# The order of the three part products in the split matmuls of a gated mix of linear attention and Fourier mixing

## The chip, the cores and the metric

The kernel runs on one core of one Trainium2 chip, in one launch. The metric is the device time of that core in microseconds (us). A profile is one execution of the program recorded by the hardware profiler; its engines are PE (TensorE matmuls), PEld (TensorE loads of stationary operands), DVE (VectorE), ACT (ScalarE), POOL (GpSimd) and SP (SyncE, which issues most DMAs).

## The reference

The inputs are `x` of 2048 tokens by 576 features, weights for a linear attention with 32 heads of 18 features, and two pairs of DFT matrices (over the sequence, 2048 x 2048, and over the features, 576 x 576). Cut to what matters:

```python
g = sigmoid((x * gate_w).sum(-1, keepdims=True))
# a: linear attention
q, k, v = split(x @ wqkv)
pq, pk = phi(q), phi(k)                  # t + 1 or exp(t)
kv = einsum("bhsd,bhse->bhde", pk, v)
z = einsum("bhsd->bhd", pk)
a = (einsum("bhqd,bhde->bhqe", pq, kv) / einsum("bhqd,bhd->bhq", pq, z)) @ wo
# b: Fourier mixing, the real part of a DFT over D and then over S
re = einsum("bsd,ed->bse", x, dft_hid_re)
im = einsum("bsd,ed->bse", x, dft_hid_im)
b = einsum("ts,bse->bte", dft_seq_re, re) - einsum("ts,bse->bte", dft_seq_im, im)
return g * a + (1 - g) * b
```

All of it is float32.

## The kernel before, in words

**Split operands.** A matmul here takes operands of the type float32r. To keep float32 precision, each operand is written as a high part (a copy rounded to that type, made by ScalarE in `hi_of`, L167) and a low part (the rest, made by VectorE in `lo_of`, L177). A product of two such operands is then three part products that add up in the same PSUM bank: high x high, high x low and low x high. `FULL` (L608) lists them in this order; the first number of a pair picks the part of the stationary operand, the second that of the moving (streamed) one. Each matmul has 128 rows, 128 columns of the stationary operand and 288 streamed columns (half of 576), except the rest of the feature dimension (below).

**Stages.** The attention comes first: key features (L512 and L197), the key-weight sums (L637), the query features and the attention output (L197 again), up to 264 us of the span. In the key features' first stage (L512), for each weight row, four matmuls stream that same row under four different stationary tiles, one for each of four token tiles. In L197 (`steps`) each contraction chunk gives high high, high low, low high, and the last chunk two matmuls, 14 in all. In L637 each of the three part products runs for both halves of 576 columns before the next, so two matmuls in a row have the same stationary tile.

Then the Fourier part runs twice, with the real and then with the imaginary matrices, and both runs have the same two steps. Each uses a fast scheme with seven products of half-sized blocks instead of eight (`PRODUCTS`, `ORDER`).

1. *The products over D* (`Hidden.run`, with `Hidden.product`; matmuls at L903). For each of 8 tiles `p` and each of the seven products there are seven matmuls into one bank: two contraction chunks `c` with three part products each, and one rest matmul of 96 rows, in which the leftover 32 features stand with their parts stacked. The stationary operand is a tile of `x` (`xf` or `xb`, high and low in the same tile), the moving one the weight `w` (`wf`, where the high and low parts of both chunks come by one transfer, L872). VectorE and ScalarE combine the seven results into the factors of the next step: a high part `fh` and a low part `fl` for each tile `p` and each form `f` (class `Factors`). For the last two tiles (6 and 7) this split is put into `backlog`, and done when the sequence products already run: ScalarE makes the high parts in batch 1, VectorE the low parts after that (`rest_lows` in batch 2).

2. *The sequence products* (`sequence`; matmuls at L1058). There are 32 batches `n`, four for each of 8 pairs of output rows. A batch covers two tiles `p` (2b and 2b + 1, where b is n modulo 4) and has, for each of the seven products and each of the two tiles, three part products: 42 matmuls. The stationary operand is a piece of the DFT matrix, `c` (high and low parts, made batch by batch), the moving one the factors. In the last pair of rows of the second run two batches are taken together. After the fourth batch of a pair the seven banks are combined, mixed with the attention rows and stored.

**What sets the order.** The order of instructions on PE, VectorE, ScalarE and SP is written out by hand in these stages: it is the order of the program text. Low parts are often put off (`lo_later`, `tick`), so that they stand behind other work of VectorE.

The lines that the change touches are L608 (beside which a second list is added), L900 in `product` and L1057 in `sequence`.

Of the kernel before, what the change touches and what calls it, by code (L numbers as in the profile page):

```python
# [14 lines left out]
P = 128  # L15
# [38 lines left out]
class Ring:  # L54
# [5 lines left out]
    def next(self):  # L60
        self.n += 1
        return self.at[(self.n - 1) % len(self.at)]
# [63 lines left out]
def kernel(  # L126
# [23 lines left out]
    def at(offset, shape, dtype=F, name="t"):  # L150
        count[0] += 1
        t = nc.alloc_sbuf_tensor_at(f"{name}_{count[0]}", list(shape), dtype,
                                    offset=base + offset)
        return t.ap()
# [8 lines left out]
    def bank():  # L163
        return psum.tile([P, 512], F, tag="bank", name="bank")
# [17 lines left out]
    def tick():  # L182
        while pending:
            pending.pop(0)()

    def add(dst, a, b, op=ALU.add):
        nc.vector.tensor_tensor(out=dst, in0=a, in1=b, op=op)  # L187
# [6 lines left out]
    def run(ps, pairs):  # L194
        pairs = list(pairs)
        for n, (a, b) in enumerate(pairs):
            nc.tensor.matmul(ps, a, b, start=(n == 0), stop=(n == len(pairs) - 1))  # L197

    def half(h):
        return slice(h * HALF, (h + 1) * HALF)  # L200
# [283 lines left out]
    for h in range(2):  # L484
        ps = [bank()[:, :HALF] for _ in range(FT)]
        parts = wkt.split(h, KC)
        for c, (raw, hi, lo) in enumerate(first):
            passes = [(hi, c), (lo, c), (hi, 5 + c)][:3 if c < KC else 2]
            tiles = [range(FT)] * len(passes)
            if h == 0 and c == 0:  # L490
                a, b = ab
# [114 lines left out]

    wvt, wot, gts = {}, [], {}
    FULL = ((0, 0), (0, 1), (1, 0))  # L608
    kv = [bank() for _ in range(3)]

    def kv_of(g):
# [16 lines left out]
    for c in range(5):  # L628
        ps = [bank(), bank()]
        passes = FULL if c < KC else FULL[:2]  # L630
        for q in range(NCU):
# [137 lines left out]
    def build_m(gs):  # L769
        for g in gs:  # L770
            n = gsize(g)
            for h in range(2):
                ps = bank()
                run(ps[:n, :HALF], [(kvb[:n, g, a, :n], wot[g][:n, b, half(h)])
                                    for a, b in FULL])
                nc.scalar.activation(mf[:n, g, half(h)], ps[:n, :HALF], AF.Copy)
# [86 lines left out]
    class Hidden:  # L863
# [33 lines left out]

        def product(self, ps, p, k, start):
            x, (w, wl) = self.x[p, k], self.w[k]
            ops = [(x[:, a, c * P:c * P + P], w[:, 2 * c + b]) for c in range(2) for a, b in FULL]  # L900
            ops.append((self.rest[p][:96, 6 - k], wl[:96]))
            for n, (a, b) in enumerate(ops):
                nc.tensor.matmul(ps, a, b, start=(start and n == 0), stop=(n == len(ops) - 1),  # L903
                                 skip_group_check=True)
# [112 lines left out]
    def sequence(m, g, src, dst, last=None, between=None):  # L1017
        late, held, stores, rest_lows = [], [], [], []
        for n in range(NP * NB):
            j, b = divmod(n, NB)  # L1020
            if b == 0:
                ps = {k: bank()[:, :HALF] for k in PRODUCTS}
                row = {t: at(mix_ring.next(), [P, D], F, "row") for t in (j, j + NP)}
                for t, a in row.items():
                    nc.sync.dma_start(out=a, in_=src[t])
            c = m.ready.pop(0)
            m.load(n + 3)
            while stores:
                stores.pop(0)()
            if n == 2:  # L1030
                tick()
            if m.raws:
                new = m.make()
                next(new)
                next(new)
                if b < NB - 1:
                    next(new, None)
            else:
                new = iter(())
                tick()  # L1040
            if n == 1:
                while backlog:
                    backlog.pop(0)()
                rest_lows += pending[-2:]
                del pending[-2:]
            elif n == 2:
                while rest_lows:
                    rest_lows.pop()()
            end = last is not None and j == NP - 1
            held.append((b, c))  # L1050
            if end and b == NB - 2:
                continue
            for q, (l, f) in PRODUCTS.items():
                for b, c in held:
                    for k in range(BS):
                        p = b * BS + k
                        for i, (x, y) in enumerate(FULL):  # L1057
                            nc.tensor.matmul(ps[q], c[x][:, l, k], factors[p](y, f),  # L1058
                                             start=(p == 0 and i == 0),
                                             stop=(p == NP - 1 and i == 2))  # L1060
            held.clear()
            if between is not None:
                between(n)
            while late:
                late.pop(0)()
            if b < NB - 1:
                continue
            y = at(Y_AT, [P, 2, 2, HALF], F, "ys")
            c11, c12, c21, c22 = (y[:, i // 2, i % 2] for i in range(4))

            def mix(t, v, h=None, g=g, row=row, store=True, end=end):
                cs = slice(0, D) if h is None else half(h)
                a = row[t][:, cs]
                nc.vector.scalar_tensor_tensor(a, v, g[:, t:t + 1], a, op0=ALU.mult, op1=ALU.add)  # L1074
                if store:
                    stores.append(lambda: nc.sync.dma_start(out=dst[t][:, cs], in_=a))
                if store and end:
                    stores.pop()()

            nc.scalar.activation(c11, ps[1], AF.Copy)  # L1080
            tick()
            add(c12, ps[6], c11, ALU.subtract)
            add(c11, ps[2], c11)
            next(new, None)
            if end:
                mix(j, c11, 0)
                add(c21, c12, ps[7], ALU.subtract)
                add(c12, ps[5], c12)
                add(c22, c12, ps[7], ALU.subtract)
                mix(j + NP, c22, 1)  # L1090
                mix(j + NP, c21, 0, store=False)
                mix(j, c12, 1, last, store=False)
                mix(j, ps[3], 1)
                mix(j + NP, ps[4], 0, last)
            else:
                add(c21, c12, ps[7], ALU.subtract)
                add(c12, ps[5], c12)
                add(c22, c12, ps[7], ALU.subtract)
                add(c12, ps[3], c12, ALU.subtract)
                add(c21, c21, ps[4], ALU.subtract)  # L1100
                late += [lambda t=t, i=i, y=y, mix=mix: mix(t, y[:, i].rearrange("p a b -> p (a b)"))
                         for i, t in enumerate((j, j + NP))]
        for f in late:
            f()
        for f in stores:
            f()
# [84 lines left out]
    mr.load(0)  # L1191
    first.run(mr, {1: 5, 2: 6, 6: 7}, {0: 5, 1: 6, 3: 7})
    sequence(mr, gate_n, att, mid, between=late)
    factors.clear()
    second.run(mi, {1: 5, 2: 6, 6: 7}, {0: 5, 1: 7})
    sequence(mi, gate_m, mid, [out[t * P:(t + 1) * P] for t in range(NT)], last=gate_n)
    paced.close()

# [87 lines left out]
```

## Time and profile before

| What | Value |
|---|---|
| Median of 3 runs | 733.61 us (733.57 to 733.9) |
| Span of the profiled execution | 730.4 us |
| Runs over the span | 3.2 us |
| Mean granted TensorE clock | 1.000 |
| PE instructions | 5,444 matmuls, 5,444 weight loads |
| Products over D, in the chain of waits | 264.15 to 316.8 us, and 501.1 to 548.3 us |
| Sequence products, in the chain of waits | 316.8 to 495.4 us, and from 548.3 us to the end |
| DMA traffic | 158.82 MB, mean 217 GB/s |

The times of runs are of executions without the profiler. The page of the profile gives no time of its own for the profiled execution but its span, from the first to the last instruction; the 3.2 us between this and the median of the runs lie outside of the span.

A row of a group reads: line, engine, operation, output tile <- input tiles, shape, count | busy us, mean ns of one | idle time of the engine just before. A matmul's duration there (some 295 ns) is longer than the distance from one start to the next, since matmuls overlap; the price of one matmul is read from a stretch: its length by its count. In a row of the timeline or of the chain stand the start in us, the length in us, and what ran, with the count of instructions that were merged. In a row of waits stand who waited, for whom, and the total, the times and the longest in us.

### The profile page before, as it was taken

To read this page: it belongs to the slowest core of one execution; us is meant where nothing else is said; L and a number is where in the kernel's file an instruction comes from. 1 tells how busy PE (TensorE), PEld (TensorE's weight loads), DVE (VectorE), ACT (ScalarE), POOL (GpSimd) and SP (SyncE) were. 2 spreads that over 40 slices of the span, in tenths; PEclk is the share of its full clock that TensorE was granted. 3 is DMA by queue.
4 is the path that set the end of the run, shared out by engine and by line. 5 is a ranking of instruction groups with operands and counts; after the bars stand their busy time and mean duration, and the time that the engine had idled before them with its cause. 6 is when DMAs were issued, how large, how long until landed. Compare 5 with 4: busy or idle time off the path is not lost.

```text
span 730.4 us, 13876 instructions
## 1 busy us (share of the span) xinstructions
PE 724.2 (99%) x5444; PEld 722.4 (99%) x5444; DVE 601.0 (82%) x995; ACT 335.6 (46%) x522; POOL 57.0 (8%) x98
## 2 busy tenths in 40 slices
PE   8999999999999999999999999999999999999998
PEld 8999999999999999999999999999999999999997
DVE  5689866779999948989899989767889988788884
ACT  6898435678644444453344334323535332232231
POOL 1011200051032110000000000000000000000000
PEclk9999999999999999999999999999999999999999
DMA  7286787677477999644475666889964544544440
GB/s 254 84 275 217 265 296 234 226 215 224 155 221 298 362 312 383 211 153 135 165 240 177 228 233 202 296 279 395 374 219 130 171 145 135 156 149 148 152 152 33
DMA packets 54356, 158.82 MB, mean 217 GB/s; under 512 B 6420, under 2 KB 11092, under 8 KB 53268
## 3 DMA queue, kind: packets, MB, share of 16 engines
q1 hardware_dynamic: 45044, 118.90, 48.7%
q0 software_dynamic: 8960, 38.65, 14.6%
q8 instruction: 43, 0.70, 0.4%
q10 hardware_dynamic: 288, 0.39, 0.2%
q14 instruction: 21, 0.17, 0.1%
HBM read 115.05 MB, written 41.39 MB: 214 GB/s over the span
## 4 chain that ended last, share of the span: by engine, by line
PE 96%; DMA 2%; DVE 1%; ACT 0%; issue 0%; SPq 0%; DVEq 0%
PE bank L1058 48%; PE bank L197 23%; PE bank L903 14%; PE bank L637 7%; PE bank L512 2%; PE bank L738 1%; DMA wraw<-in_wk_dram 1%; DMA wf<-wm 1%; DMA craw<-in_xg_dram 1%; PE bank L619 0%; DVE row L1074 0%; ACT xb L167 0%; DVE ys L187 0%; PE bank L622 0%; ACT wd L167 0%
## 5 line engine op out<-in xcount | busy, mean ns | idle before, releaser
L1058 PE MATMUL bank<-fh,c 128*128 128x288 f32 x1792 | 357.5, 295 | 0.0
L1058 PEld LDWEIGHTS bank<-fh,c 128*128 128x128 f32 x1792 | 287.5, 188 | 0.0
L1058 PE MATMUL bank<-fl,c 128*128 128x288 f32 x896 | 264.2, 295 | 0.0
L167 ACT ACTIVATE c<-craw 128x1792 fp32r<-128x1792 f32 (+1 forms) x84 | 121.4, 1447 | 187.1 <-DVE craw L187 166.3
L1058 PEld LDWEIGHTS bank<-fl,c 128*128 128x128 f32 x896 | 168.9, 189 | 0.0
L177 DVE TENSOR_TENSOR c<-craw,c 128x1792 fp32r<-128x1792 f32 (+4 forms) x86 | 142.0, 1653 | 5.9 <-ACT c L167 5.7
L187 DVE TENSOR_TENSOR craw<-craw 128x256 f32<-128x256 f32 (+1 forms) x192 | 98.3, 512 | 25.2 <-DMA craw<-in_ci_dram 12.7
L197 PE MATMUL bank<-wd,xs 128*128 128x288 f32 (+1 forms) x784 | 106.3, 296 | 0.4 <-ACT wd L167 0.4
L197 PEld LDWEIGHTS bank<-wd,xs 128*128 128x128 f32 x784 | 104.7, 188 | 0.6 <-ACT wd L167 0.6
L903 PE MATMUL bank<-wf,xf 128*128 128x288 f32 x588 | 92.1, 297 | 0.2 <-DMA wf<-wm 0.2
L903 PEld LDWEIGHTS bank<-wf,xf 128*128 128x128 f32 x588 | 84.0, 189 | 0.4 <-issue 0.4
L197 PE MATMUL bank<-mw,qs 128*128 128x288 f32 x448 | 63.2, 297 | 0.0
L637 PE MATMUL bank<-pk,c 128*128 128x288 f32 x448 | 61.1, 296 | 0.1
L637 PEld LDWEIGHTS bank<-pk,c 128*128 128x128 f32 x448 | 59.9, 189 | 0.3 <-DVE c L177 0.3
L197 PEld LDWEIGHTS bank<-mw,qs 128*128 128x128 f32 x448 | 59.9, 188 | 0.2 <-DVE qs L177 0.2
L187 DVE TENSOR_TENSOR ys<-bank,ys 128x288 f32<-128x288 f32 x63 | 28.8, 457 | 16.1 <-PE bank L1058 12.4
L336 DVE SCALAR_TENSOR_TENSOR acc<-bank,e 128x288 f32<-128x288 f32 x64 | 28.3, 454 | 15.2 <-ACT e L335 13.7
L177 DVE TENSOR_TENSOR fl<-fl,fh 128x864 fp32r<-128x864 f32 (+1 forms) x32 | 34.6, 1093 | 7.1 <-ACT fh L167 5.8
L167 ACT ACTIVATE fh<-fl 128x864 fp32r<-128x864 f32 (+1 forms) x32 | 29.8, 950 | 16.2 <-DVE fl L187 16.2
L903 PE MATMUL bank<-wf,xr 96*128 96x288 f32 x112 | 33.3, 298 | 0.0
L1123 ACT ACTIVATE acc<-bank,gate 128x288 f32<-128x288 f32 x32 | 16.0, 500 | 35.1 <-PE bank L197 34.8
L187 DVE TENSOR_TENSOR ys<-ys,bank 128x288 f32<-128x288 f32 x47 | 21.2, 450 | 12.6 <-PE bank L1058 12.0
(107 smaller groups left out, 665.9 us busy)
## 6 DMA issues: line engine op xcount, KB each, us to landing
xf<-xm SPq DMA_DIRECT2D x42, 512.0 KB, 7.9
craw<-in_cr_dram SPq DMA_DIRECT2D x32, 512.0 KB, 4.1
craw<-in_ci_dram SPq DMA_DIRECT2D x32, 512.0 KB, 3.5
xraw<-in_xa_dram SPq DMA_DIRECT2D x28, 320.0 KB, 4.3
xm<-xb POOLq DMA_DIRECT2D x8, 1024.0 KB, 5.9
wf<-wm SPq DMA_DIRECT2D x14, 576.0 KB, 5.4
xr<-xr SPq DMA_DIRECT2D x14, 448.0 KB, 8.0
xm<-xb POOLq DMA_DIRECT2D x8, 768.0 KB, 5.9
```

The lines of the kernel that those rows point to most:

```text
L167: return nc.scalar.activation(dst, src, AF.Copy, bias=bias)
L177: nc.vector.tensor_tensor(out=dst, in0=src, in1=hi, op=ALU.subtract)
L187: nc.vector.tensor_tensor(out=dst, in0=a, in1=b, op=op)
L197: nc.tensor.matmul(ps, a, b, start=(n == 0), stop=(n == len(pairs) - 1))
L336: nc.vector.scalar_tensor_tensor(dst, ps, 0.0, e, op0=ALU.max, op1=ALU.add)
L512: nc.tensor.matmul(ps[i], x[:, i * P:(i + 1) * P], wkt.row(h, j), start=(c == 0 and n == (0 if h or i < 2 else 2)), stop=(c == KC and n == 1))
L637: nc.tensor.matmul(ps[h][:, :HALF], t[:, a, k], pk[s][:, b, half(h)], start=(s == 0 and n == 0), stop=(s == NT - 1 and n == len(passes) - 1))
L738: nc.tensor.transpose(banks[c // KC][:, (c % KC) * P:(c % KC + 1) * P], a, ident)
L903: nc.tensor.matmul(ps, a, b, start=(start and n == 0), stop=(n == len(ops) - 1), skip_group_check=True)
L1058: nc.tensor.matmul(ps[q], c[x][:, l, k], factors[p](y, f), start=(p == 0 and i == 0), stop=(p == NP - 1 and i == 2))
L1123: done.append(nc.scalar.activation(acc[i][:, half(h)], ps[:, :HALF], AF.Copy, scale=gate[:, i:i + 1]))
```

## The change

A second list, `TURN`, has the same three part products with the first two exchanged: high low, high high, low high. The products over D use it for both chunks of every product. The sequence products use it in all batches but the first of each run (`n` is 0 there, and `b` is 0 too as no other batch is held). Everything else is as it was.

```diff
     FULL = ((0, 0), (0, 1), (1, 0))
+    TURN = ((0, 1), (0, 0), (1, 0))
...
         def product(self, ps, p, k, start):
             x, (w, wl) = self.x[p, k], self.w[k]
-            ops = [(x[:, a, c * P:c * P + P], w[:, 2 * c + b]) for c in range(2) for a, b in FULL]
+            ops = [(x[:, a, c * P:c * P + P], w[:, 2 * c + b]) for c in range(2) for a, b in TURN]
...
                         p = b * BS + k
-                        for i, (x, y) in enumerate(FULL):
+                        for i, (x, y) in enumerate(TURN if n or b else FULL):
                             nc.tensor.matmul(ps[q], c[x][:, l, k], factors[p](y, f),
                                              start=(p == 0 and i == 0),
                                              stop=(p == NP - 1 and i == 2))
```

## The prediction

> **What bounds the kernel now.** The first view is the page's table of busy time, with the slices under it.
>
> ```profile
> PE 724.2 (99%) x5444; PEld 722.4 (99%) x5444; DVE 601.0 (82%) x995; ACT 335.6 (46%) x522; POOL 57.0 (8%) x98
> PEclk9999999999999999999999999999999999999999
> ```
>
> TensorE works for 99% of the span of 730.4 us, in 5,444 matmuls with as many weight loads, and its granted clock is full in every slice. VectorE follows at 82%. Busy time on PE is modelled, so the second view is the chain of waits, in order of time. Its pieces say how long a stretch of matmuls took from its start to what followed, and so what one of them costs.
>
> ```profile
> 21.13 44.55 PE bank L197 x336
> 65.67 19.17 PE bank L637 x144
> 130.90 2.09 PE bank L637 x16
> 264.15 52.63 PE bank L903 x392
> 316.79 178.61 PE bank L1058 x1344
> 495.39 0.02 issue
> 495.41 5.60 DMA wf<-wm
> 501.01 0.14 issue
> 501.14 47.15 PE bank L903 x350
> 548.29 175.38 PE bank L1058 x1320
> ```
>
> The two stretches of L1058 (the sequence products) and of L903 (the products over D), which the change touches, make up 178.61 + 175.38 + 52.63 + 47.15 = 453.8 us of the chain. One sequence product matmul takes 178.61 / 1344 = 132.9 ns in the first run and 175.38 / 1320 = 132.9 ns in the second. The third view is who waited for whom, on PE.
>
> ```profile
> PE bank L223 <- POOL ones_f L219: 1.2, 1, 1.2
> PE bank L512 <- ACT wd L167: 0.6, 1, 0.6
> PE bank L197 <- ACT wd L167: 0.4, 1, 0.4
> PE bank L903 <- DMA wf<-wm: 0.2, 1, 0.2
> ```
>
> That is 2.4 us in all, none of it in L1058. The 5.60 us of a transfer in the chain lie under other matmuls; PE stood for 0.2 us of it. So in the touched stages the time is the number of matmuls times the price of one. A reordering can act only through that price, or through a wait which comes earlier.
>
> **The change, part by part.** Nothing is added or removed. Line 900 gives 7 products x 8 tiles x 2 chunks x 2 runs = 224 triples. Line 1057 gives 42 matmuls in each of 31 batches (all but the first) in each of 2 runs: 2,604 matmuls, or 868 triples. Together 1,092 triples, 3,276 matmuls, change their order from high high, high low, low high to high low, high high, low high. In the built program these swaps and the waits that go with them are all that differs; the rows of VectorE, ScalarE, GpSimd and of both DMA-issuing engines stand in the same order.
>
> The groups by form show that the work per matmul stays:
>
> ```profile
> L1058 PE MATMUL bank<-fh,c 128*128 128x288 f32 x1792 | 357.5, 295 | 0.0
> L1058 PE MATMUL bank<-fl,c 128*128 128x288 f32 x896 | 264.2, 295 | 0.0
> L1058 PEld LDWEIGHTS bank<-fh,c 128*128 128x128 f32 x1792 | 287.5, 188 | 0.0
> L1058 PEld LDWEIGHTS bank<-fl,c 128*128 128x128 f32 x896 | 168.9, 189 | 0.0
> ```
>
> Every matmul has its own load of the stationary operand, also where it repeats the one before (the first two of a triple share c high in both orders): 1,792 + 896 loads for 2,688 matmuls. The loads of high, high, low come in the same order as before. What moves is the streamed factor: high, low, high becomes low, high, high. So the second and third matmul of a triple now stream the same tile one after the other. The price of such a repeat is the first unknown.
>
> *Its bounds.* The nearest row is the stage at L512, where four matmuls in a row (one for each of four token tiles) stream the same weight row under different stationary tiles. Its stretch without a wait, from the timeline:
>
> ```profile
> 13.29 7.84 PE L512 MATMUL bank<-wd,xs 128*128 128x288 f32 x58
> ```
>
> With one duration of 0.29 us taken off for the last matmul's own length, (7.84 - 0.29) / 57 = 132.4 ns from start to start. Three of four pairs there repeat the streamed operand, and it is no dearer than the stages that hardly repeat it: 132.6 at L197 (44.55 / 336) and 132.9 at L1058. The dearest stretch with whole tiles and no rest rows among the quoted is L637, 19.17 / 144 = 133.1 ns. So the price of the changed matmuls lies between 0.5 ns under and 0.2 ns over today's: over all 3,276 of them, -1.6 to +0.7 us. I take the row that it is nearest to, L512, for the matmul that becomes a repeat: 1,092 x -0.5 ns = -0.5 us. L903 has 134.3 ns (52.63 / 392), with rest matmuls of 96 rows after every six whole ones; those stay where they are.
>
> The Trainium skill, "TensorE: Matmul & The Clock Gate", section "Back-to-back issue gap", gives N / 2.4 + 2.5 ns for an isolated warm matmul, which is an estimate of 122.5 ns for 288 columns, 10.4 ns below this trace's 132.9. If a repeated streamed operand got rid of that whole difference, 1,092 repeats would bring 11.4 us and the time would be 722; the L512 stretch, at 132.4 ns, speaks against it.
>
> *The waits.* In the old order the low factor is read by the second matmul of a triple, now by the first, one matmul (0.13 us) sooner. In the products over D, low and high weights come with the same transfer, so nothing changes there. In the sequence products the low factors of the last two tiles are made late, by VectorE, shortly before batch 3 reads them. A low factor that came too late would hold up every matmul behind it, since PE's matmuls start in program order all through the trace, and the products' readers on ScalarE and VectorE in turn. The start of batch 3 is 126 matmuls after the first start of L1058:
>
> ```profile
> L1058 PE MATMUL bank<-fh,c x1792: 292/295/302, 316.6 to 726.6; 128*128 128x288 f32 x200
> 331.40 2.32 DVE L177 TENSOR_TENSOR fl<-fl,fh 128x1152 fp32r<-128x1152 f32 x2
> 333.26 0.43 PE L1058 MATMUL bank<-fh,c 128*128 128x288 f32 x2
> 334.72 0.29 PE L1058 MATMUL bank<-fl,c 128*128 128x288 f32 x1
> 563.41 2.32 DVE L177 TENSOR_TENSOR fl<-fl,fh 128x1152 fp32r<-128x1152 f32 x2
> 565.17 0.42 PE L1058 MATMUL bank<-fh,c 128*128 128x288 f32 x2
> 566.62 0.29 PE L1058 MATMUL bank<-fl,c 128*128 128x288 f32 x1
> ```
>
> 316.6 + 126 x 0.1329 = 333.4 us, the second matmul of the row at 333.26. The last low factor (tile 7, forms 4 to 6) is done at 331.40 + 2.32 = 333.72 us. It was first read by the matmul at 334.72, and will be by the one before it in place, at 334.59: 0.87 us of room, 0.73 if the wait sits on the weight load, which runs a matmul ahead. In the second run the same operation ends at 565.73 and is read at 566.62 - 0.13 = 566.49: 0.76 us, or 0.63 with the load. Work that covers it: the nine matmuls of the batch before that read. If VectorE were later by more than the room, PE would stand for the excess alone, once in each run. I count 0.
>
> *The sum.* 730.4 us of span - 0.5 = 729.9. The three runs have a median of 733.61, which is 3.2 us over the span and lies around the program; so 733.1 us.
>
> **The rivals.**
>
> *A repeat is clearly cheaper (faster).* The fastest stretch in the chain is the one at 130.90: 2.09 us for 16 matmuls, 130.6 ns. If the repeated streamed operand brings a matmul down to this, 1,092 x 2.3 ns = 2.5 us go, and the time is 731.1; if the whole triple ran so, 3,276 x 2.3 = 7.5 us and 726.1. For it: prices of one and the same shape do differ between stages. Against it: 16 matmuls are few, that stretch repeats no streamed operand, and L512, which does, stays at 132.4.
>
> *A repeat is dearer (slower).* Place: the third matmul of each triple, which reads the tile that the second is still streaming. For it: L637 repeats the stationary operand in 3 of 6 pairs and takes 133.1 ns, L197 in 4 of 14 and takes 132.6. That is (133.1 - 132.6) / (0.500 - 0.286) = 2.3 ns for a repeat. If a repeat of the streamed operand costs the same, the change makes 1,092 more of them: +2.5 us, 736.1. It decides from 1.5 / 1,092 = 1.3 ns for a repeat on. Against it: L512 again, with three repeats in four and the lowest price of the long stretches.
>
> *The change does nothing to the order.* Excluded: the built program has the swap in every triple named above. It would give 733.6, which is inside the likeliest case anyway.
>
> **How the numbers follow.** No measurable change, around 733.1 and between 732.0 and 734.3 by the bounds above: 0.58, since the one stage that has the new pattern shows no other price. Cheaper repeat, around 731.1: 0.24. Dearer repeat, around 736.1: 0.18; the two are not less likely because a difference of 1.3 ns in 133 is below what separates the stages, so no row can exclude it. 0.2% of 733.6 is 1.5 us, about what a measurement of this kernel can tell from no change; the first case lies almost wholly within it, the second beyond it on the fast side, the third on the slow side. So faster 0.24, same 0.58, slower 0.18. For 8 in 10 the range takes in half of each of the two rivals: 731.0 to 735.8.
>
> **What would show it.** In the profile of the changed kernel: a chain piece of L1058 with 1,344 matmuls in 178.0 to 178.8 us, and the L903 pieces at 134 ns (step one right); below 176.6 us, which is 131.4 ns a matmul, the cheaper repeat; above 179.5, the dearer. PE's waits without a row of L1058 on an L177 operation (the room held); such a row would mean that batch 3 waits for its low factors. DVE, ACT and DMA counts must be the same. The prediction is wrong if the pitch of the triple changes by more than 1.3 ns per triple, for whatever reason, since I have only one stage of 58 matmuls for the pattern that is now made 1,092 times.

## The result, and the profile after

| | Before | After |
|---|---|---|
| Median of 5 runs each, side by side | 733.57 us (732.58 to 733.9) | 729.53 us (728.65 to 729.7) |
| Ratio, with its 95% interval | | 0.9939 [0.9927, 0.995] |
| Span of the profiled execution | 730.4 us | 727.8 us |

The change makes the kernel 4.04 us faster, 0.6%. The forecast was 733.1 us with a range from 731.0: the time lies 1.5 us below the range.

The profiled execution of after took 729.53 us in all, so 1.7 us lie outside its span. Before, the prediction set its span of 730.4 us against a median that is 3.2 us higher. In 21 later runs of the kernel before, 1.7 to 1.8 us lie outside the span, so that execution took about 732.1 us by this estimate, some 1.4 us under the median. The two spans therefore differ by 2.6 us, and the medians by 4.0.

The page of after, with the table of busy time and the granted clock:

```profile
span 727.8 us, 13876 instructions
PE 720.8 (99%) x5444; PEld 718.9 (99%) x5444; DVE 600.6 (83%) x995; ACT 335.5 (46%) x522; POOL 57.2 (8%) x98
PEclk9999999999999999999999999999999999999999
```

The same instructions, the same full clock, the same engine at 99%. PE is busy for 3.4 us less (724.2 before). Five rows of the chain of waits of after (start, length, what ran):

```profile
268.04 49.42 PE bank L904 x371
317.47 177.16 PE bank L1059 x1344
494.65 5.62 DMA wf<-wm
500.40 46.66 PE bank L904 x350
547.07 173.99 PE bank L1059 x1320
```

Lines have moved down by one: L904 are the products over D, L1059 the sequence products. Against the pieces of before with the same counts, the sequence products lost 178.61 - 177.16 = 1.45 us and 175.38 - 173.99 = 1.39 us. The 350 matmuls of the products over D lost 47.15 - 46.66 = 0.49 us, 1.4 ns each. Who waited on PE, after:

```profile
PE bank L223 <- POOL ones_f L219: 1.2, 1, 1.2
PE bank L904 <- DMA wf<-wm: 1.0, 2, 0.7
PE bank L197 <- ACT wd L167: 0.5, 1, 0.5
PE bank L638 <- DVE c L177: 0.3, 1, 0.3
PE bank L512 <- ACT wd L167: 0.3, 1, 0.3
```

The waits are 3.3 us in all, 0.9 more than before. So nothing was gained from waits; the gain is in the price of a matmul. The view by stretches shows it most plainly. It counts PE's matmuls (x) in two stretches of 160 us inside the sequence products, in which PE never stood still. First before, then after; the columns are named in the first line.

```profile
core 0: us, PE busy (x), PEclk, DMA share, GB/s
320.00:480.00 160.00, 160.00 (x1206) 1.00 0.59 201
552.00:712.00 160.00, 160.00 (x1207) 1.00 0.45 148
```

```profile
320.00:480.00 160.00, 160.00 (x1216) 1.00 0.60 204
552.00:712.00 160.00, 160.00 (x1216) 1.00 0.43 145
```

Ten matmuls more in the same time, at the same clock and with nearly the same load on the DMA engines.

For a finer measure I take the start times of the matmuls in the trace. A *batch* below is the time from the first matmul of a batch of sequence products to the first of the next, 42 matmuls; a *tile* is the same for the 49 matmuls of one tile in the products over D. The steady ones repeat to the nanosecond:

```
                      before                        after
batch, run 1          5611, 5580, 5580, 5580 ...    5534, 5613, 5533, 5533, 5534 ...
batch, run 2          5611, 5580, 5580, 5580 ...    5534, 5612, 5534, 5533, 5533 ...
tile (steady)         6573                          6493
```

A steady batch is 47 ns shorter (132.9 to 131.7 ns a matmul), a steady tile 80 ns. Not every tile is steady: the seven tiles behind the first lost 0.49 us in the first run and 0.47 in the second, 1.4 ns a matmul, which by estimate makes 1.1 us for all 784 matmuls. With the 1.45 + 1.39 us of the sequence products that is 3.9 us, about the difference of the medians. One detail does not fit a price per changed matmul: batch 0, whose order was not changed, is also 77 ns shorter. That detail decides something below.

### The profile page after: what moved, and what is told of

Same layout as the page of the kernel before. It is cut to its first block, busy times and chain, and to the rows that moved or that the text cites. A ratio compares the mean times of both kernels' runs of the same rounds, so it can differ in the third digit from the quotient of the medians.

```text
span 727.8 us, 13876 instructions
## 1 busy us (share of the span) xinstructions
PE 720.8 (99%) x5444; PEld 718.9 (99%) x5444; DVE 600.6 (83%) x995; ACT 335.5 (46%) x522; POOL 57.2 (8%) x98
## 4 chain that ended last, share of the span: by engine, by line
PE 86%; issue 5%; DMA 4%; DVE 3%; POOL 1%; ACT 1%; SPq 0%; DVEq 0%; POOLq 0%
PE bank L1059 48%; PE bank L197 15%; PE bank L904 13%; PE bank L638 7%; PE bank L512 2%; DMA wf<-wm 1%; DMA wraw<-in_wk_dram 1%; DMA craw<-in_xg_dram 1%; DMA att<-acc 1%; POOL att L1126 1%; DVE qs L177 0%; PE bank L620 0%; DVE pz L709 0%; DVE den L710 0%; DVE wb L177 0%
## 5 line engine op out<-in xcount | busy, mean ns | idle before, releaser
L1059 PE MATMUL bank<-fh,c 128*128 128x288 f32 x1792 | 354.6, 294 | 0.0
L1059 PEld LDWEIGHTS bank<-fh,c 128*128 128x128 f32 x1792 | 286.7, 188 | 0.0
L1059 PE MATMUL bank<-fl,c 128*128 128x288 f32 x896 | 263.6, 294 | 0.0
L1059 PEld LDWEIGHTS bank<-fl,c 128*128 128x128 f32 x896 | 168.7, 188 | 0.0
L177 DVE TENSOR_TENSOR c<-craw,c 128x1792 fp32r<-128x1792 f32 (+4 forms) x86 | 141.9, 1653 | 5.7 <-ACT c L167 5.6
L197 PE MATMUL bank<-wd,xs 128*128 128x288 f32 (+1 forms) x784 | 106.3, 296 | 0.5 <-ACT wd L167 0.5
L197 PEld LDWEIGHTS bank<-wd,xs 128*128 128x128 f32 x784 | 104.7, 188 | 0.7 <-ACT wd L167 0.6
L904 PE MATMUL bank<-wf,xf 128*128 128x288 f32 x588 | 91.1, 295 | 0.2 <-DMA wf<-wm 0.2
L904 PEld LDWEIGHTS bank<-wf,xf 128*128 128x128 f32 x588 | 83.3, 189 | 0.4 <-issue 0.4
L197 PE MATMUL bank<-mw,qs 128*128 128x288 f32 x448 | 63.2, 297 | 0.0
L197 PEld LDWEIGHTS bank<-mw,qs 128*128 128x128 f32 x448 | 59.9, 188 | 0.2 <-DVE qs L177 0.2
L177 DVE TENSOR_TENSOR fl<-fl,fh 128x864 fp32r<-128x864 f32 (+1 forms) x32 | 34.6, 1092 | 6.9 <-ACT fh L167 5.7
L904 PE MATMUL bank<-wf,xr 96*128 96x288 f32 x112 | 33.3, 298 | 0.0
```

Source lines behind the costliest of these rows:

```text
L177: nc.vector.tensor_tensor(out=dst, in0=src, in1=hi, op=ALU.subtract)
L1059: nc.tensor.matmul(ps[q], c[x][:, l, k], factors[p](y, f), start=(p == 0 and i == 0), stop=(p == NP - 1 and i == 2))
```

## The experiments

Unless said otherwise the kernel of an experiment was run once, beside one run of the kernel before on the same chip. Single times of this kernel differ by more than a microsecond from run to run, so the verdicts on single runs rest on the batches, not on the times.

**All orders of the three parts, in the sequence products alone.** Five kernels that leave the products over D in the old order, and put another list in the sequence products (first number stationary, second streamed):

```diff
-                        for i, (x, y) in enumerate(FULL):
+                        for i, (x, y) in enumerate(PARTS if n or b else FULL):
...
+    PARTS = ((0, 1), (0, 0), (1, 0))    # e1: high low, high high, low high
+    PARTS = ((1, 0), (0, 0), (0, 1))    # e2: low high, high high, high low
+    PARTS = ((0, 0), (1, 0), (0, 1))    # e3: high high, low high, high low
+    PARTS = ((0, 1), (1, 0), (0, 0))    # e4: high low, low high, high high
+    PARTS = ((1, 0), (0, 1), (0, 0))    # e5: low high, high low, high high
```

> The new order (high low, high high, low high) in the sequence products alone; the products over D as before. All theories below were formed on this order, so all say the same: a sequence matmul takes 131.8 ns (before 132.9), the first stretch of 1,344 some 177.2 us (before 178.6), the products over D stay at 52.6 us for 392. The run is some 2.9 us faster than before.

> Sequence products in the order low high, high high, high low; products over D as before. Theory A (a matmul that streams the same tile as the one before it is cheaper, by 3.2 ns): one such repeat in a triple, 131.8 ns a matmul. Theory B (it is what the triple begins with, the low streamed part): 132.9. Theory C (what costs is a step at which both operands change; one such step in a triple fewer than before): 131.8. Theory D (what costs is streaming the low factor while the low stationary part is loaded): 132.9, since here the low factor is streamed last and the next triple's low part is loaded under it.

> Sequence products in the order high high, low high, high low; products over D as before. Theory A (repeat of the streamed tile): one repeat, 131.8 ns a matmul. Theory B (begins with the low streamed part): 132.9. Theory C (steps at which both operands change): two in a triple as before, 132.9. Theory D (low factor streamed while the low stationary part is loaded): does not occur here, 131.8.

> Sequence products in the order high low, low high, high high; products over D as before. Theory A (repeat of the streamed tile): one repeat, 131.8 ns a matmul. Theory B (begins with the low streamed part): 131.8. Theory C (steps at which both operands change): two in a triple as before, 132.9. Theory D (low factor streamed while the low stationary part is loaded): occurs once in a triple as before, 132.9.

> Sequence products in the order low high, high low, high high; products over D as before. The earlier orders gave for a repeated batch of 42 matmuls 5,580 ns (high low in the middle), 5,533 (high low first, two orders) and 5,553 (high low last, two orders), to the ns whatever the stationary parts did. If the time hangs on the sequence of streamed tiles alone, this order (high, low, high, as before the change) gives 5,580 again. If it hangs on the stationary order too (theory D, or a saving where the stationary part repeats), it gives another number.

```
                     streamed tiles     steady batch   time (before on that chip)
before (hh hl lh)    high low high      5580           
e5     (lh hl hh)    high low high      5580           732.95 (732.87)
e1     (hl hh lh)    low high high      5533           731.46 (732.91)
e4     (hl lh hh)    low high high      5533           731.65 (732.91)
e2     (lh hh hl)    high high low      5553           730.73 (732.91)
e3     (hh lh hl)    high high low      5553           731.96 (732.91)
```

The six orders fall into three pairs, and the two of a pair agree to the nanosecond. What they share is the order of the streamed tiles; the stationary tiles repeat in some and not in others. So which stationary tile is loaded after which has no part in the price, which excludes the theories C and D of the expectations. B foretold 132.9 ns for e2 and e3, and the repeat of the streamed tile (A) 131.8; they have 132.2. A is the nearest, but it doesn't say why one repeat in a triple is worth 47 ns a batch in e1 and e4 and 27 in e2 and e3. The stretches of e1, in which the new order stands in the sequence products alone:

```profile
320.00:480.00 160.00, 160.00 (x1216) 1.00 0.61 206
552.00:712.00 160.00, 160.00 (x1216) 1.00 0.45 149
```

That is the count of the changed kernel. The waits of e4 on PE:

```profile
PE bank L1060 <- DVE fl L177: 0.9, 1, 0.9
PE bank L1060 <- DVE c L177: 0.8, 1, 0.8
```

Here L1060 (the sequence products) waits for a low factor. Batches 2 and 3 of the second run took 6,606 and 6,894 ns; the ones after came back to 5,533, but for one of 5,613. The room that the prediction worked out for this read is thin.

**The repeat by itself.** Three kernels stream other tiles under unchanged stationary ones, in all batches but the first: one and the same tile in a whole batch (e7), two in turns (e8), fourteen one after the other (e9). They leave the other factors out of the sum, so their output is not the reference's, and neither is that of e10 and e14 below; only the prices are of interest. `at_n` counts the matmuls of a batch; the lines that count are left out here and below.

```diff
-                            nc.tensor.matmul(ps[q], c[x][:, l, k], factors[p](y, f),
+                            w = factors[p](y, f) if n == 0 else factors[b * BS](0, 3)                       # e7
+                            w = factors[p](y, f) if n == 0 else factors[b * BS](at_n % 2, 3)                # e8
+                            w = factors[p](y, f) if n == 0 else factors[b * BS](at_n // 7 % 2, at_n % 7)    # e9
+                            nc.tensor.matmul(ps[q], c[x][:, l, k], w,
```

> In all batches but the first of each run every one of the 42 sequence matmuls streams one and the same tile (a high factor of the batch's first tile); the other factors are left out of the sum. Theory A (a repeat of the streamed tile is cheaper by 3.4 ns than a step to another): all steps but those between batches are repeats, 129.5 ns a matmul, 5,440 for a batch. Theory J (each step has a price by the distance between where one read ends and the next begins, and the repeat is one of the cheap ones): below 5,533, down to some 5,440. Theory P (the place of the low part product in the triple, by its number in the program): 5,580 as before, since the program's places are those of before.

> In all batches but the first of each run the 42 sequence matmuls stream two tiles in turn, the high and the low factor of one form of the batch's first tile; the others are left out of the sum. No repeat, and only the steps high to low (start to start +8,064 bytes) and low to high (-8,064). Theory A: no repeat, so 132.9 ns a matmul, 5,580 for a batch. Theory J: half of the steps have one price, half the other; between 5,480 and 5,680.

> In all batches but the first of each run the 42 sequence matmuls stream the 14 factors of the batch's first tile one after the other as they lie in memory, three times through; the other tile's factors are left out, and the products are not the reference's. No repeat, but 13 of 14 steps begin where the read before ended. Theory A: 132.9 ns a matmul, 5,580 for a batch. Theory J, with near steps cheap: at or below the one-tile run (5,440).

The stretches of e7:

```profile
320.00:480.00 160.00, 160.00 (x1202) 1.00 0.60 203
552.00:712.00 160.00, 160.00 (x1202) 1.00 0.45 147
```

Nothing but repeats is dearer than the old order: batches of 5,598 and 5,602 ns in turns, 133.3 ns a matmul. e8, without any repeat, has 5,596 and 5,604, and e9 5,595 and 5,605. The three times were 734.94, 733.43 and 734.42 us against 732.87 before. The repeat falls too, as the cheap thing (it foretold 5,440 for e7) and as the dear one.

**Which tile.** The streamed tiles differ in where they start. One form takes 1,152 bytes of a partition, four and a half times 256, and in the built program the memory that holds them begins at byte 1,152. So half of the 112 tiles start on a multiple of 256 bytes (M below) and half start 128 bytes past one (A). e10 streams 48 pairs of tiles, each pair in turns through one batch of its own (`calls` counts the two runs).

```diff
...
+                            w = factors[p](y, f)
+                            if 4 <= n < 28:
+                                tp, ty, tf = PAIRS[len(calls) - 1][n - 4][at_n % 2]
+                                w = factors[tp](ty, tf)
```

> In batches 4 to 27 of each run the 42 sequence matmuls of a batch stream two factor tiles in turn, another pair in each batch (48 pairs: near and far, within the 16,128 bytes of one tile's factors and in two different tiles' factors, even and odd forms); the sum is not the reference's there. Theory J (distance; the runs that kept to one tile's factors had 5,600 ns a batch whatever the step): pairs in two different tiles' factors are cheaper than 5,600, pairs in one tile's are at 5,600. Theory M (the distance modulo 1,024 bytes or less decides): in-tile runs had all such distances, so nearly all pairs are at 5,600, and the saving in the real orders comes from elsewhere. Theory A (repeat): has fallen, it would give 5,580 and more for all pairs here.

From start to start within a batch, matmuls 4 to 40, in ns (time 733.86 us, before 734.13):

```
A with A (16 pairs, 18 to 882 lines of 128 bytes apart)         131.67
M with M (10 pairs)                                             133.33
A first, M second (11 of 13 pairs)                              133.33
M first, A second (9 pairs)                                     132.97 in 7, 133.33 in 2
the other two with A first:
  tile 4 low form 1 (A), tile 5 high form 1 (M)                 130.00
  tile 4 low form 1 (A), tile 7 high form 3 (M)                 132.92
```

The distance between two tiles plays no part: 18 lines cost the same as 882. The start within 256 bytes does. But it is not a fixed price per kind: one pair of A and M had 130.00. e11, next, shows that one and the same row of matmuls can have more than one steady price, which would allow this; why this pair alone had it is not explained.

**Products over D alone.** The other half of the change, the sequence products in the old order throughout.

```diff
-                        for i, (x, y) in enumerate(TURN if n or b else FULL):
+                        for i, (x, y) in enumerate(FULL):
```

> The new order in the products over D alone; sequence products as before. By the profile after the change: 132.6 ns a matmul between waits in the products over D (before 134.0) and 132.9 in the sequence products, so 784 x 1.4 = 1.1 us faster than before, and with the run that had the sequence products alone the whole 4.0 us. If the two parts were not additive (a wait that one brings), the sum would miss 4.0 by more than 0.5.

```profile
320.00:480.00 160.00, 160.00 (x1216) 1.00 0.61 204
552.00:712.00 160.00, 160.00 (x1216) 1.00 0.44 146
```

That was unexpected. The untouched sequence products have the count of the changed kernel: 5,535 in batch 0, 5,533 in all others, in both runs. The time was 729.77 us (before 734.13). The very same instructions, in the same order and at the same addresses, can so run at 5,580 or at 5,533 a batch, and what ran ahead of them decides. e10 shows the same without any change in the products over D: its last batches of each run, in the old order again, take 5,611, 5,580 and 5,580 behind the pairs of the first run, and 5,574, 5,540 and 5,534 behind those of the second.

**The addresses moved.** e12 is the old order with the low factors of forms 4 to 6 laid before those of forms 0 to 3, e13 the changed kernel with the same layout. No instruction changes but in its addresses.

```diff
-                at_a = o + (7 + a) * HALF * 4
+                at_a = o + (7 + (0 if a else 3)) * HALF * 4
```

> The old order everywhere, but the low factors of forms 4 to 6 are laid before those of forms 0 to 3, so that for forms 0 to 3 the low tile starts at the same place within 256 bytes as the high one (for forms 4 to 6 it stays 128 bytes off). Theory S (the sequence of starts within 256 bytes of the streamed tiles sets the price; pairs that both start 128 past a multiple took 131.7 ns, nearly all others 133.3): a batch of the sequence products is not at 5,580 any more. Theories of repeat or of distance: 5,580, since no tile is repeated here and the steps are of the same kind.

> The new order everywhere with the same layout as the run before. Theory S: for forms 0 to 3 the order of the parts no longer changes the sequence of starts, so new and old order differ only by what forms 4 to 6 bring: some 3/7 of 47, 20 ns a batch, instead of 47. Theory of repeat: the new order is 47 ns a batch below the old one here too.

The stretches of e12, then of e13:

```profile
320.00:480.00 160.00, 160.00 (x1211) 1.00 0.61 205
552.00:712.00 160.00, 160.00 (x1211) 1.00 0.44 149
```

```profile
320.00:480.00 160.00, 160.00 (x1199) 1.00 0.59 201
552.00:712.00 160.00, 160.00 (x1200) 1.00 0.45 146
```

With the moved addresses the sign turns: the old order takes 5,560 a batch and the new one 5,613 (133.6 ns, the dearest steady price of all runs), though the new order had the cheap products over D ahead of it (6,493 a tile). Times 732.44 and 733.01 us, before 732.29. The expectation had the new order 20 ns below the old one here, as if each form brought its own share; that missed, in sign too. So the order of high and low as such is not what pays; it pays through the addresses.

**The starts copied.** If the starts are what matters, other tiles with the same row of starts must give the same price. e14 streams 24 rows of 42 starts, each for two batches, from 24 high tiles, twelve of each kind.

```diff
...
+                            if 4 <= n < 28:
+                                odd = STARTS[12 * len(calls) - 12 + (n - 4) // 2][at_n] == "M"
+                                w = factors[at_n % 4](0, 2 * (at_n % 3) + odd)
```

> In batches 4 to 27 of each run the sequence matmuls stream high factors of tiles 0 to 3, chosen only by their start within 256 bytes (even forms start 128 past a multiple, odd ones on it), by 24 lists of 42 starts, two batches each; the sum is not the reference's there. Theory S: the lists that copy the starts of the old order, the new order and the order with the low part last give again 5,580, 5,533 and 5,553 ns, though other tiles are streamed and no repeat is kept; all odd 5,600, all even 5,530. Theory of repeat or of distance: these lists differ little from one another, since all stream ever changing tiles. The other lists are to find a sequence that costs less than 5,533.

```
the starts of ...                               first, second batch   the real thing
the old order           AMAAMAAMAAMAMAMMAMMA..  5580, 5580            5580 (before)
low high high           MAAMAAMAAMAAAMMAMMAM..  5575, 5533            5575, 5533 (e1)
high high low           AAMAAMAAMAAMMMAMMAMM..  5606, 5556            5557, 5553 (e2)
old order, products
  1 2 6 5 3 7 4         AMAAMAMAMMAMAMAAMAMA..  5541, 5533            not yet run
all M                                           5602, 5598            5603, 5598 (e7)
A and M in turns                                5595, 5605            5595, 5605 (e9)
all A                                           5528, 5532
17 other rows                                   5527 to 5633
```

The copies meet the real batches to 3 ns, but for one first batch. This also settles e7: twelve tiles that all start on M cost the same as one such tile repeated. And a row's price is not the sum of its neighbours': low high high mixes all four kinds of neighbours, and lies 1 ns off the row of A alone. The time was 732.70 us (before 732.29).

**A forecast from it.** e15 keeps the old order of parts and exchanges products instead, with the row of starts that gave 5,533 above.

```diff
-PRODUCTS = {1: (4, 0), 6: (2, 4), 2: (6, 1), 5: (1, 3), 7: (0, 5), 3: (3, 2), 4: (5, 6)}
+PRODUCTS = {1: (4, 0), 2: (6, 1), 6: (2, 4), 5: (1, 3), 3: (3, 2), 7: (0, 5), 4: (5, 6)}
```

> The old order of the parts everywhere; only the seven sequence products are taken in another order, so that even and odd forms alternate (0, 1, 4, 3, 2, 5, 6 instead of 0, 4, 1, 3, 5, 2, 6). Theory S: its list of starts is one that took 5,533 ns a batch in the run of lists, so 131.7 ns a matmul, and 64 x 47 = 3.0 us off: a ratio of 0.996, less what the end loses because the seventh product comes one later (up to 0.8 us). Theory of repeat: nothing is repeated, 5,580 a batch and no gain.

Its batches are 5,540, 5,533, 5,533, 5,534 and so on: the forecast price, with not one part product exchanged. The time didn't follow: 732.63 us, ratio 0.999 [0.9978, 1.0002]. The waits of e15 say why:

```profile
PE bank L1058 <- DVE fl L177: 0.9, 1, 0.9
PE bank L197 <- ACT wd L167: 0.5, 1, 0.5
PE bank L1058 <- DVE c L177: 0.3, 1, 0.3
```

PE waits for a late low factor and for a late low part of the matrix (batch 3 of the second run: 6,700 ns; batch 29 of the first: 6,140). In this order some factors are read sooner than VectorE has them. All the dearer batches of this execution together stand 2.6 us above 5,533, against the 3.0 us (64 x 47 ns) that the price brought.

**A further version, and the changed kernel again.** e16 is the changed kernel with the halves interleaved in L637 (so that its streamed tiles come in another order), and in the attention output; e17 is the changed kernel as it is. Both were run with e15, beside 21 runs of before.

```diff
...
+                for h in (0, 1, 0, 0, 1, 0, 1, 0, 1, 1, 0, 1) if c < KC else (0, 1, 0, 0, 1, 0, 1, 1):
+                    s, n = todo[h].pop(0)
+                    a, b = passes[n]
+                    nc.tensor.matmul(ps[h][:, :HALF], t[:, a, s - q * CU], pk[s][:, b, half(h)],
```

> The changed kernel with the two halves of the columns interleaved in the key-weight sums and in the attention output, in the list of starts A M A A M A M A M M A M (A starts 128 past a multiple of 256 bytes, M on it) instead of A M A M and of 14 A, then 14 M. Theory S: the key-weight sums go from 133.1 to 131.8 ns (384 matmuls, -0.5 us) and the attention output from 132.6 to 131.8 (448, -0.35 us): some 0.8 us below the changed kernel, ratio to before 0.993. Otherwise: no difference to the changed kernel, or slower where a half that ends later holds up ScalarE.

> The changed kernel as it is, on the same chip, for comparison: ratio 0.994 to 0.995.

e16: 729.62 us, 0.9958 [0.9941, 0.9974]; e17: 729.98 us, 0.9956 [0.9943, 0.9969]. L637 went from 133.1 ns to between 131.6 and 132.0, as forecast (131.8), over 448 matmuls some 0.5 us, which these intervals can't show. The attention output hardly moved (132.5, not the 131.8 forecast). e16 is not better than the changed kernel by anything that was measured. In e17 a stall in batch 29 of the first run (5,746 ns) was followed by 5,534.

**What runs ahead.** e18 takes e11 further down: the new order only in the last of the eight tiles of the products over D, the 49 matmuls (42 and the 7 rests) that run just before the sequence products. e19 is e11 again, with more rounds.

```diff
-            ops = [(x[:, a, c * P:c * P + P], w[:, 2 * c + b]) for c in range(2) for a, b in FULL]
+            ops = [(x[:, a, c * P:c * P + P], w[:, 2 * c + b]) for c in range(2) for a, b in (TURN if p == NP - 1 else FULL)]
```

> The new order in the products over D of the last of the 8 tiles alone (42 matmuls before each run of sequence products); all else in the old order. Theory S with entry (the list of starts allows more than one steady course, and what ran before decides which): the sequence products with their old order take 5,533 to 5,540 ns a batch from batch 0 on, as in the run with all products over D changed; the first seven tiles stay at 6,573 ns for 49 matmuls. 64 x 47 = 3.0 us off, ratio 0.996. Theory S with the list alone: 5,580 a batch, no gain beyond 0.2 us.

> The new order in the products over D alone, timed. By its first profile 16 tiles x 80 ns = 1.3 us in the products over D and 64 x 47 = 3.0 us in the sequence products: ratio 0.994, the same as the whole change (0.9939), so that the sequence part brings nothing more where the products over D have the new order.

e18, its stretches:

```profile
320.00:480.00 160.00, 160.00 (x1217) 1.00 0.61 204
552.00:712.00 160.00, 160.00 (x1217) 1.00 0.44 147
```

One changed tile ahead is enough: 5,534, 5,533 and so on from batch 0, in both runs, with the other seven tiles at the old 6,573. Its time was 732.03 us, 0.9978 [0.9968, 0.9988], 1.3 us less where 3.0 were expected, and its 11 values lie in two groups (four from 730.25 to 730.82, seven from 731.74 to 732.63); the profiled execution is one of the first group. e19: 730.43 us, 0.9954 [0.9938, 0.997]. Its profiled execution shows what can happen to such a run. First the chain, then the wait on PE:

```profile
315.99 99.62 PE bank L1059 x756
...
452.60 2.03 DVE c L177
454.68 39.06 PE bank L1059 x292
```

```profile
PE bank L1059 <- DVE fl L177: 0.8, 1, 0.8
```

```
e19, run 1, batches 23 to 28    5534, 5533, 5931, 5580, 5580, 5580
e19, run 2, batches 1 to 6      5533, 5533, 6844, 5580, 5594, 5580
```

In the first run PE resumes behind VectorE's `c` at 454.68 us, in batch 25; in the second it waits 0.8 us for a low factor in batch 3. After either, the old order goes on at 5,580 to the end of the run. The new order came back to 5,533 after its stalls (e4, e17).

## Why the prediction was wrong

**What bounds the kernel: right.** PE, by number of matmuls times their price. No instruction, transfer or clock changed, and the whole gain is in the price.

**The bounds of the price: the step that failed.** "So the price of the changed matmuls lies between 0.5 ns under and 0.2 ns over today's", taken from the averages of other stages, with L512 as the row for a repeated streamed tile. Measured: 1.1 ns under in the sequence products, 1.4 in the products over D, -3.9 us instead of -0.5. It failed in two ways. L512 was taken because it repeats streamed tiles (in 48 of 57 pairs of the quoted stretch, not three of four, since a weight row is streamed under the high and then under the low tiles), and the repeat is not what matters (e7, e14). And averages of stages bound nothing here, as each stage has its own row of starts: steady batches went from 131.7 to 133.6 ns with the same shape and count.

The profile before already held both prices. In the built program L512 streams tiles of one start (A or M) for twelve and more matmuls in a row, then tiles of the other, and so does the attention output in some of its rows. I take eight steps from start to start inside such runs, from the fourth step on. L512 has 131.75 ns in two runs of A and 133.25 in two of M; the attention output has 131.6 to 131.8 in four runs of A and 133.3 to 133.9 in four of M. The 132.4 of the L512 row mixes the two; it is not the price of a repeat. The prediction asked which tile repeats; where the tiles lie in memory, which the kernel's layout tells, it did not ask. Nor could a price per changed matmul tell that the unchanged batch 0 would gain 77 ns.

The prediction's own sign of being wrong, more than 1.3 ns for a triple, was met: 47 ns over the 14 triples of a batch are 3.4 ns for each.

**What the new price comes from.** Shown for the sequence products: the row of starts within 256 bytes of the streamed tiles sets the steady price (copied in e14, turned in e13, foretold in e15). For the old row there are two steady prices, 5,580 and 5,533, and what ran before decides which (e11, e18), or a stall (e19). So the parts of the change don't add up. The products over D bring some 1.1 us of their own and, by what they leave behind, the gain of the sequence products as well; the new order in the sequence products brings that gain from either entry (e1, e17). What the second adds to the first is argued, not shown: it comes back after a stall, where the old order stays dear. The medians of e19 (0.9954) and of the whole change (0.9939 and 0.9956) can't be told apart.

**The waits: right, with little to spare.** After has no row of L1059 on an L177 operation, as forecast. The room was there, but e4, e15 and e19, in each of which the same factors were late once, show waits of 0.8 to 0.9 us at that place. The waits that did grow, 0.8 us of them for `wf` at the start of the products over D, are elsewhere, and are smaller than the differences between executions.

**The sum.** Its 3.2 us "around the program" are 1.7; the rest is that the profiled execution was a quick one. It didn't move the forecast, which ends at the median again.

**The rivals.** "A repeat is clearly cheaper" had the sign, and with 2.5 us more than half of the size; its reason, that some stretches of one shape do cost less, holds, and its mechanism is refuted by e7. "A repeat is dearer" was argued from L637 and L197, with a wrong count: L637 repeats its stationary tile in 4 of 6 pairs, not 3, which would have made the slope 1.3 ns. That slope means nothing, as e1 and e4 differ in their stationary order and not in price. A slower outcome was possible all the same: in the layout of e13 the same edit costs 53 ns a batch (5,613 against 5,560). The 722 us worked out from the issue gap is as far off as the L512 row said.

## What to carry to other kernels

In a stage that TensorE bounds, read the price of a matmul from start to start, batch by batch, before and after any edit that only reorders: a price that repeats to the nanosecond and moves by 0.8% is a finding, and an average over stages hides it. When operands of one stage start at different places within 256 bytes, treat their order and their layout as something to try on the chip, several rows at a time as in e14, and not to forecast from the kind of operand. Look also at what such a stage inherits: here an edit of 42 matmuls ahead of a stage made 1,344 untouched ones cheaper, and one stall could take it back. Before a stage's average is taken as the price of a pattern, see whether its single steps have one price.

## What the runs showed of the hardware

- Matmuls of 128 x 288 float32r with a weight load each ran at steady prices from 131.7 to 133.6 ns for whole batches (but for one pair, below), with nothing different but the starts of their streamed tiles and what ran ahead. Tiles that start 128 bytes past a multiple of 256: 131.67 ns; on a multiple: 133.33. The tiles that L512 and the attention output stream show the same two prices within 0.6 ns. Which of the two is cheap may hang on something that no run varied (the place in the arena, the type, 288 columns).
- One row of matmuls had two steady prices, 5,580 and 5,533 ns for 42, and stayed on either for over a hundred microseconds until something disturbed it.
- One pair of tiles ran at 130.00 ns, the lowest price seen over a batch, and a pair of the same kinds of start at 133.33. What makes the difference is open, as is the mechanism behind all of it, whether e12 and e13 have a second steady price as well, and what parts the two groups of e18's times. That the products over D gain by the starts of their weights is likely but was not tried.
- The Trainium skill, "TensorE: Matmul & The Clock Gate", section "Back-to-back issue gap", lets the price of a matmul go by its numbers of columns. Its formula for an isolated warm matmul is an estimate of 122.5 ns for 288, and no batch here came below 130.0 ns a matmul. The Trainium skill, "SBUF — State Buffer", section "Operand start alignment", asks that an operand start at a multiple of its element size, and says of its own measurements that they are about legality and timed nothing. The runs here timed such starts: between some that are all legal lie up to 1.9 ns of a matmul's 133.
